# A cosine from one sine with a quarter turn, its rounding on VectorE and its square removed

## The chip, the cores and the metric

One core of one Trainium2 chip runs the whole kernel. The metric is device time in microseconds (us) from one launch; a run's profile gives the span from the first to the last instruction.

## The reference: sliding-window attention feeding g = h cos(h)

Eight batches, 8 heads of 64, 512 local and 32 global tokens. Local queries see the local keys within 32 positions and all global keys; global queries see everything. The result x, 4352 tokens of 512, goes through two products with a cosine between them.

```
s_g = scale * q_g @ [k_g, k_l].T ;  out_g = sm(s_g) @ [v_g, v_l]
s_ll = where(|i - j| <= 32, scale * q_l @ k_l.T, -1e9) ;  s_lg = scale * q_l @ k_g.T
out_l = sm([s_lg, s_ll]) @ [v_g, v_l]
x = concat(out_g, out_l) as (8*544, 512)
h = x @ w_in          # w_in 512 x 2048
g = h * cos(h)
out = g @ w_out       # w_out 2048 x 512
```

## The kernel before

Every fp32 product is formed from fp16 pairs: a value is split into a high half (`xh`, `wi_h`, `gh`, ...) and what is left (`xl`, `wi_l`, `gl`, ...), and three products of halves are summed in PSUM. Powers of two scale each operand, so that the halves fit fp16.

**Attention** is worked for pairs of heads, (batch, pair) from (0,0) to (7,3). PE forms scores `ps` (L573, from batch 3 on L560 with split operands). DVE adds the mask and takes the minimum (L633, tiles `t` and `mn`), ACT takes Exp with sums `sm` (L450), DVE forms reciprocals (L652, L653). ACT writes the high planes (L680) and DVE the low ones (L681), two heads each for four windows. DMA transposes the planes into `pt` (by PE in batch 0). PE sums with the values into `acc` (L733). ACT and DVE evict it as `xh` (L753) and `xl` (L754). Global queries have tiles of their own (`gt`, `planes_g`, `gacc`, `xg`, L796 to L859). Values are split once per batch (`vm` L507, `vl` L538), queries and keys from batch 3 on per pair (`qh` on ACT L614, `qkr` on DVE L617).

**The two products** go by chunks of 256 tokens (16, and one more for the global tokens) and in each by 8 slots of 2x128 hidden columns. A slot has these steps, with the chunk's scales `a`, `m`, `o` in tiny columns (L890 to L894, one set for two chunks):

- `m1_a` (L909): 24 products into the PSUM tile `ph`, three buffers; here h is `ph` times a scale.
- `m1_b`: ACT writes u = ph + m (L931), where m is a large constant that rounds the sum; DVE then forms u = (u - m) - ph (L932), the distance to the nearest period.
- `m1_c`: ACT takes w = Sin(a u) (L937, recorded at L450).
- `m1_d`: GpSimd squares w in four pieces (`pool_tt`, recorded at L238); DVE forms gf = (w - 0.5) ph (L955); ACT casts the high half `gh` (L959); GpSimd forms the low half `gl` in four pieces (L238).
- `m2_a` (L978): 12 products with `w_out` into `po`, which has two buffers, one for each 128 tokens. They come three slots after their `m1_a`, and are called a W_out group below.
- `m2_b`, `m2_c`: after the eighth slot ACT (L989) and DVE (L987) scale `po` into `o`, and a DMA writes it.

So a slot's `ph` is held until gf has read it, and with three `ph` buffers (two slots ahead) the chain u, Sin, square, gf is in the loop that lets PE go on. `w_out` is itself decoded beside the first two chunks: loads into two buffers (`raw_wo`, L427), conversion steps on ACT, DVE and GpSimd (L252, L253, L257, L264, L238) into `wo_hl`.

The order on each engine is set in two steps. The program lists every step under a slot and a phase with `at(...)`, which gives it a priority; a scheduler then simulates the engines with its own costs and fixes one order per engine. A change of one step's engine or length therefore moves steps on all engines. Exp and Sin share ACT, and `table_act` keeps their order, so that function tables are loaded seldom.

```
            nc.scalar.activation(u, ph, AF.Identity, bias=m)                       # L931
            nc.vector.scalar_tensor_tensor(u, u, m, ph, op0=ALU.subtract, ...)     # L932
                pool_tt(w, w, w, ALU.mult, PSQ if c < 2 else PSC)                  # L953
```

Of the kernel before, what the change touches and what calls it, by code (L numbers as in the profile page):

```python
# [145 lines left out]
def body(tc, qf, v, wi, wo, mask, out):  # L146
# [3 lines left out]
    with ExitStack() as ctx:  # L150
# [791 lines left out]
        def m1_d(c, j):  # L942
# [4 lines left out]
            e = SQ[NS * c + j] if c < 2 else "G"  # L947
            if e == "A":
                nc.scalar.activation(w, w, AF.Square)
            elif e == "D":  # L950
                nc.vector.tensor_tensor(w, w, w, op=ALU.mult)
            else:
                pool_tt(w, w, w, ALU.mult, PSQ if c < 2 else PSC)  # L953
# [265 lines left out]
```

## Time and profile before

| | |
|---|---|
| median of 3 runs | 938.96 us (938.77 to 941.5) |
| profiled execution | 938.54 us |
| its span | 936.7 us |
| PE busy | 883.8 us (94%) |
| DVE busy | 648.1 us (69%) |
| ACT busy | 683.0 us (73%) |
| GpSimd busy | 540.6 us (58%) |
| mean granted TensorE clock | 0.966 |

PE is TensorE's products, DVE VectorE, ACT ScalarE, POOL GpSimd. An engine's share is a mean over stages that have different limits, so it is read by stretch: up to about 190 us both weights are decoded and the first two batches' attention runs; then up to about 760 us attention of batches 2 to 7 runs beside the products; after that the products run alone. A line of waits names the engine that stood idle, the tile it was to write, and the instruction that ended last of those it waited for.

### The profile page before, as it was taken

The numbers are of one execution on the slowest core, as the hardware profiler recorded it, in microseconds if no ns is written. First come the engines' busy times: TensorE is split into PE (matmuls) and PEld (weight loads), VectorE is DVE, ScalarE is ACT, GpSimd is POOL, SyncE is SP. The second block draws the span as 40 slices with busy tenths as digits, with TensorE's granted clock in tenths as the row PEclk, the third lists the DMA queues.
The fourth block names the chain that finished last, engine by engine and source line by source line (L and its number), as shares of the span: only waits on it lengthen the run. The fifth ranks groups of instructions, "written<-read, shape, count | busy, mean of one in ns | idle before, by whom it ended". The sixth has DMA issues, their size and how long they took to land.

```text
span 936.7 us, 21428 instructions
## 1 busy us (share of the span) xinstructions
PE 883.8 (94%) x7903; PEld 596.1 (64%) x7903; DVE 648.1 (69%) x1708; ACT 683.0 (73%) x1439; POOL 540.6 (58%) x1228
## 2 busy tenths in 40 slices
PE   6756888999999999999999999999999999999995
PEld 4445554666666666666666666666666666666762
DVE  5999989857576777778877878687776664323231
ACT  6887798876787788877888788788877785434341
POOL 5866968543546555545646364546464556555552
PEclk8568998999999999999999999999999999999998
DMA  9936257555232543545343645362434333000000
GB/s 366 392 140 191 69 145 176 115 116 142 50 104 51 153 85 69 115 125 113 69 112 62 164 61 122 60 175 47 99 67 93 51 69 61 23 1 24 1 23 23
DMA packets 155185, 96.50 MB, mean 103 GB/s; under 512 B 141000, under 2 KB 141128, under 8 KB 153288
## 3 DMA queue, kind: packets, MB, share of 16 engines
q1 hardware_dynamic: 155080, 95.13, 40.4%
q8 instruction: 62, 1.02, 0.4%
q14 instruction: 43, 0.35, 0.1%
HBM read 51.59 MB, written 8.91 MB: 65 GB/s over the span
## 4 chain that ended last, share of the span: by engine, by line
PE 73%; DVE 10%; ACT 6%; DMA 4%; POOL 4%; issue 3%; SPq 0%; ACTq 0%; POOLq 0%
PE ph L909 32%; PE po L978 32%; PE acc L733 3%; PE ps L560 3%; DMA vr<-v 2%; DVE planes L681 2%; ACT t L450 1%; DMA raw_wo<-wo 1%; DVE u L932 1%; PE gacc L838 1%; ACT planes L680 1%; PE gps L783 1%; PE ps L573 1%; DVE gf L955 1%; POOL w L238 1%
## 5 line engine op out<-in xcount | busy, mean ns | idle before, releaser
L238 POOL TENSOR_TENSOR gl<-gf,gh 128x128 f16<-128x128 f32 x544 | 233.2, 463 | 180.6 <-ACT gh L959 180.6
L978 PE MATMUL po<-wo_hl,gh 128*128 128x512 f16 x1088 | 322.3, 381 | 9.6 <-POOL wo_hl L238 9.0
L238 POOL TENSOR_TENSOR w<-w 128x128 f32<-128x128 f32 x544 | 214.4, 426 | 168.6 <-ACT w L450 166.7
L909 PE MATMUL ph<-xh,wi_h 128*128 128x256 f16 x1024 | 280.4, 274 | 3.3 <-DVE gf L955 3.1
L909 PE MATMUL ph<-xl,wi_h 128*128 128x256 f16 x1024 | 279.5, 273 | 0.5 <-DVE xl L754 0.5
L909 PE MATMUL ph<-xh,wi_l 128*128 128x256 f16 x1024 | 279.4, 273 | 0.0
L909 PEld LDWEIGHTS <-wi_h 128*128 128x128 f16 x2176 | 207.3, 98 | 51.6 <-issue 12.7
L978 PE MATMUL po<-wo_hl,gl 128*128 128x512 f16 x544 | 201.5, 381 | 0.0
L978 PEld LDWEIGHTS <-gh 128*128 128x128 f16 x1088 | 106.8, 98 | 103.2 <-issue 2.8
L955 DVE SCALAR_TENSOR_TENSOR gf<-w,ph 128x512 f32<-128x512 f32 x136 | 93.0, 684 | 93.2 <-POOL w L238 92.3
L931 ACT ACTIVATE u<-ph,cm 128x512 f32<-128x512 f32 x136 | 91.7, 678 | 79.0 <-PE ph L909 79.0
L450 ACT ACTIVATE w<-u,ca 128x512 f32<-128x512 f32 x136 | 98.0, 721 | 65.1 <-DVE u L932 57.8
L932 DVE SCALAR_TENSOR_TENSOR u<-u,cm,ph 128x512 f32<-128x512 f32 x136 | 100.7, 740 | 64.6 <-ACT u L931 64.6
L959 ACT CAST gh<-gf 128x512 f16<-128x512 f32 x136 | 83.1, 611 | 55.9 <-DVE gf L955 53.5
L450 ACT ACTIVATE t<-t,mn 128x192 f32<-128x192 f32 (+1 forms) x256 | 116.5, 457 | 6.2 <-DVE mn L633 5.9
L909 PEld LDWEIGHTS <-wi_l 128*128 128x128 f16 x1088 | 106.8, 98 | 13.4 <-issue 0.7
L681 DVE SCALAR_TENSOR_TENSOR planes<-t,sm,planes 128x192 f16<-128x192 f32 (+1 forms) x232 | 95.4, 464 | 6.7 <-ACT planes L680 6.5
L978 PEld LDWEIGHTS <-gl 128*128 128x128 f16 x544 | 53.4, 98 | 73.2 <-issue 11.1
L680 ACT ACTIVATE planes<-t,sm 128x192 f16<-128x192 f32 (+1 forms) x232 | 86.9, 455 | 2.9 <-DVE gsm L810 2.2
L450 ACT ACT_TABLE_LOAD x58 | 74.4, 1283 | 6.7 <-DVE u L932 4.6
L633 DVE CUSTOM_DVE_ANT_0 t<-ps,msk,qs 128x192 f32<-128x192 f32 (+1 forms) x160 | 60.2, 428 | 3.1 <-PE ps L560 3.1
L733 PE MATMUL acc<-pt,vh 128*64 128x128 f16 (+3 forms) x768 | 45.5, 239 | 3.0 <-ACT pt L698 3.0
(173 smaller groups left out, 1116.0 us busy)
## 6 DMA issues: line engine op xcount, KB each, us to landing
qkr<-qf SPq DMA_DIRECT2D x31, 608.0 KB, 5.0
vr<-v SPq DMA_DIRECT2D x8, 1280.0 KB, 6.5
out<-o SPq DMA_DIRECT2D x34, 256.0 KB, 2.0
raw_wi<-wi SPq DMA_DIRECT2D x6, 1024.0 KB, 12.3
wo_hl<-wo SPq DMA_DIRECT2D x8, 512.0 KB, 11.4
raw_wm<-wo SPq DMA_DIRECT2D x8, 512.0 KB, 4.4
raw_wo<-wo SPq DMA_DIRECT2D x8, 512.0 KB, 4.4
raw_wi<-wi SPq DMA_DIRECT2D x4, 512.0 KB, 12.2
```

What stands on the lines that cost most here:

```text
L238: nc.gpsimd.tensor_tensor(o[..., c], a[..., c], b[..., c], op=op)
L450: ins = nc.scalar.activation(*a, **k).ins
L633: nc.vector.tensor_tensor_reduce(t[:, h], pt[h], msk[:, MOFF[i] : MOFF[i] + w], nal, 3.0e38, ALU.add, ALU.min, mn[:, h : h + 1],)
L680: a = nc.scalar.activation(hi, t[:, h], AF.Identity, scale=r)
L681: d = nc.vector.scalar_tensor_tensor(lo, t[:, h], r, hi, op0=ALU.mult, op1=ALU.subtract)
L733: mm = nc.tensor.matmul(acc[64 * h : 64 * h + 64, q_out : q_out + n0 * len(segs)], vt[:, tl, 64 * h : 64 * h + 64], rhs, start=(k == 0 and ...
L909: nc.tensor.matmul(ph[:, a], w[:, kc, f], x[:, kc, q], start=first and ip == 0, stop=last and ip == 2, skip_group_check=True,)
L931: nc.scalar.activation(u, ph, AF.Identity, bias=m)
L932: nc.vector.scalar_tensor_tensor(u, u, m, ph, op0=ALU.subtract, op1=ALU.subtract)
L955: nc.vector.scalar_tensor_tensor(gf, w, 0.5, st.pop(("ph", c, j)).rearrange("p a b -> p (a b)"), op0=ALU.subtract, op1=ALU.mult,)
L959: nc.scalar.copy(gh, gf)
L978: nc.tensor.matmul(po[k], g[:, a * CT + k * P : a * CT + (k + 1) * P], w[:, 2 * j + a], start=(j == 0 and i == 0), stop=(j == NS - 1 and i ...
```

## The change

The cosine is formed by cos(h) = sin(quarter turn - h) in place of 1 - 2 sin(h/2) squared. The rounding goes by whole periods with an offset q of an eighth of m's unit. In order:

- u = (ph + q) + m is one DVE operation that reads PSUM, with two scalar columns; it was an ACT operation. The second pass stays as it was (L933 now).
- Sin has scale -2 pi/period in place of pi/period, and the column `halfpi` as bias. That column is written once at the start; it shares a tile with `pvs`.
- The square is removed, with its constants `PSQ` and `SQ`.
- gf = (-0.5 w) ph in place of (w - 0.5) ph, the same operation with other constants.
- The scales are columns of one tile `cs`, with two more tiny operations per set.

```
--- before.py
+++ after.py
@@ -74,9 +74,7 @@
 LO = "m01v2345"
 J7 = "xl3"
 L7 = -5
-PSQ = 128
 PSG = 128
-SQ = "GGGGGGGGGGGGGGGG"
 GLE = "GGGGGGGGGGGGGGGG"
 WLE = "GGGGGGGGGGGGGGGG"
 WPT = [1, 1, 2, 2, 3, 3, 4, 4, 5, 5, 6, 6, 7, 7, 8, 8]
@@ -183,7 +181,9 @@
         hsc = cp.tile([P, 1], F32, name="hsc")
         osc = cp.tile([P, 1], F32, name="osc")
         xg = cp.tile([P, B, NPAIR, SG], F32, name="xg")
-        pvs = cp.tile([P, B], F32, name="pvs")
+        pvs_hp = cp.tile([P, B + 1], F32, name="pvs_hp")
+        pvs, halfpi = pvs_hp[:, :B], pvs_hp[:, B : B + 1]
+        nc.vector.memset(halfpi, math.pi / 2)
 
         def behind(ins, what, why="scale_first"):
             if st.get(what) is not None:
@@ -884,15 +884,16 @@
                     )
                 st["x", c] = (xh, xl)
 
-            a = ap_.tile([P, 1], F32, tag="ca", name=f"ca_{c}")
-            m = ap_.tile([P, 1], F32, tag="cm", name=f"cm_{c}")
-            o = ap_.tile([P, 1], F32, tag="co", name=f"co_{c}")
+            cs = ap_.tile([P, 4], F32, tag="cs", name=f"cs_{c}")
+            a, m, o, q = (cs[:, i : i + 1] for i in range(4))
             nc.vector.tensor_scalar(a, hsc, pv, None, op0=ALU.mult)
             inv2(m, a)
-            nc.vector.tensor_scalar(m, m, 2.0**90, 0.5 * MAGIC, op0=ALU.min, op1=ALU.mult)
-            nc.vector.tensor_scalar(a, a, math.pi, None, op0=ALU.mult)
+            nc.vector.tensor_scalar(m, m, 2.0**90, None, op0=ALU.min)
+            nc.vector.tensor_scalar(q, m, 0.125, None, op0=ALU.mult)
+            nc.vector.tensor_scalar(m, m, MAGIC / 2, None, op0=ALU.mult)
+            nc.vector.tensor_scalar(a, a, -2.0 * math.pi, None, op0=ALU.mult)
             nc.vector.tensor_scalar(o, osc, pv, None, op0=ALU.mult)
-            st["cs", c] = (a, m, o)
+            st["cs", c] = (a, m, o, q)
 
 
         def m1_a(c, j, part=None):
@@ -928,13 +929,13 @@
                 u = mp.tile([P, n], F32, tag="u", name=f"u_{c}_{j}")
                 w = mp.tile([P, n], F32, tag="w", name=f"w_{c}_{j}")
             m = st["cs", c][1]
-            nc.scalar.activation(u, ph, AF.Identity, bias=m)
+            nc.vector.tensor_scalar(u, ph, st["cs", c][3], m, op0=ALU.add, op1=ALU.add)
             nc.vector.scalar_tensor_tensor(u, u, m, ph, op0=ALU.subtract, op1=ALU.subtract)
             st["u", c, j] = (u, w)
 
         def m1_c(c, j):
             u, w = st["u", c, j]
-            ins = table_act("Sin", w, u, AF.Sin, scale=st["cs", c][0])
+            ins = table_act("Sin", w, u, AF.Sin, scale=st["cs", c][0], bias=halfpi)
             x = st.pop("new_x", None)
             if c and x is not None:
                 tc.add_manual_dep(ins, x.name, order, reason="products_first")
@@ -944,17 +945,10 @@
             n = w.shape[-1]
             gh = mp.tile([P, n], F16, tag="gh", name=f"gh_{c}_{j}", bufs=GB)
             gl = mp.tile([P, n], F16, tag="gl", name=f"gl_{c}_{j}", bufs=GB)
-            e = SQ[NS * c + j] if c < 2 else "G"
-            if e == "A":
-                nc.scalar.activation(w, w, AF.Square)
-            elif e == "D":
-                nc.vector.tensor_tensor(w, w, w, op=ALU.mult)
-            else:
-                pool_tt(w, w, w, ALU.mult, PSQ if c < 2 else PSC)
             gf = gf_tile(c, j, n)
             nc.vector.scalar_tensor_tensor(
-                gf, w, 0.5, st.pop(("ph", c, j)).rearrange("p a b -> p (a b)"),
-                op0=ALU.subtract, op1=ALU.mult,
+                gf, w, -0.5, st.pop(("ph", c, j)).rearrange("p a b -> p (a b)"),
+                op0=ALU.mult, op1=ALU.mult,
             )
             nc.scalar.copy(gh, gf)
             if c < 2 and GLE[NS * c + j] == "D":
```

Three places show what the order does. In names such as `u_1_6_2499` the first numbers are chunk and slot (for `ps`, `t`: batch, pair, window), the last is a count.

On DVE where the products begin, before:

```order
L434 TENSOR_REDUCE wm_o_1010<-wos_108 128x1
L435 TENSOR_SCALAR wm_o_1010<-wm_o_1010 128x1
L932 SCALAR_TENSOR_TENSOR u_0_0_1209<-u_0_0_1209,cm_0_1202,ph_0_0_1038 128x512
L211 TENSOR_SCALAR wm_o_1010<-wm_o_1010 128x1
L932 SCALAR_TENSOR_TENSOR u_0_1_1227<-u_0_1_1227,cm_0_1202,ph_0_1_1045 128x512
```
and with the change:

```order
L932 TENSOR_SCALAR u_0_0_1210<-ph_0_0_1039,cs_0_1202 128x512
L434 TENSOR_REDUCE wm_o_1011<-wos_109 128x1
L932 TENSOR_SCALAR u_0_1_1224<-ph_0_1_1046,cs_0_1202 128x512
L933 SCALAR_TENSOR_TENSOR u_0_0_1210<-u_0_0_1210,cs_0_1202,ph_0_0_1039 128x512
L435 TENSOR_SCALAR wm_o_1011<-wm_o_1011 128x1
L933 SCALAR_TENSOR_TENSOR u_0_1_1224<-u_0_1_1224,cs_0_1202,ph_0_1_1046 128x512
L211 TENSOR_SCALAR wm_o_1011<-wm_o_1011 128x1
```
Each slot has a TENSOR_SCALAR (L932) and a SCALAR_TENSOR_TENSOR (L933) now, and the passes of two slots stand among the scale steps of w_out (`wm_o`).

On DVE at the end of batch 1's attention, where the low planes of pair (1,3) are written, before:

```order
L681 SCALAR_TENSOR_TENSOR planes0_76<-t_1_3_0_2223,sm_1_3_2374,planes0_76 128x192 x2
L681 SCALAR_TENSOR_TENSOR planes1_78<-t_1_3_1_2227,sm_1_3_2374,planes1_78 128x224 x2
L955 SCALAR_TENSOR_TENSOR gf_1_4_2392<-w_1_4_2311,ph_1_4_2285 128x512
L681 SCALAR_TENSOR_TENSOR planes2_80<-t_1_3_2_2237,sm_1_3_2374,planes2_80 128x224 x2
L858 TENSOR_SCALAR xg_97<-gacc_1_0_2331,pvs_98 128x64
L681 SCALAR_TENSOR_TENSOR planes3_82<-t_1_3_3_2241,sm_1_3_2374,planes3_82 128x192 x2
L859 SCALAR_TENSOR_TENSOR xg_97<-gacc_1_0_2331,pvs_98,xg_97 128x64
L816 SCALAR_TENSOR_TENSOR planes_g_84<-gt_1_1_2096,gsm_1_1_2383,planes_g_84 128x544
L538 SCALAR_TENSOR_TENSOR vl_2_1_2685<-vr_2_1620,vs_2_1788,vh_2_1_2684 128x640
L538 SCALAR_TENSOR_TENSOR vl_2_2_3084<-vr_2_1620,vs_2_1788,vh_2_2_3083 128x640
```
and with the change:

```order
L949 SCALAR_TENSOR_TENSOR gf_1_5_2467<-w_1_5_2374,ph_1_5_2348 128x512
L681 SCALAR_TENSOR_TENSOR planes0_76<-t_1_3_0_2180,sm_1_3_2327,planes0_76 128x192 x2
L681 SCALAR_TENSOR_TENSOR planes1_78<-t_1_3_1_2184,sm_1_3_2327,planes1_78 128x224 x2
L681 SCALAR_TENSOR_TENSOR planes2_80<-t_1_3_2_2194,sm_1_3_2327,planes2_80 128x224
L932 TENSOR_SCALAR u_1_7_2570<-ph_1_7_2545,cs_0_1202 128x512
L681 SCALAR_TENSOR_TENSOR planes2_80<-t_1_3_2_2194,sm_1_3_2327,planes2_80 128x224
L681 SCALAR_TENSOR_TENSOR planes3_82<-t_1_3_3_2198,sm_1_3_2327,planes3_82 128x192
L633 ISA t_2_0_2_2528,mn_2_0_2_2529<-ps_2_0_2_0_2515,msk_73 128x224
L633 ISA mn_2_0_2_2529 128x1
L633 ISA t_2_0_2_2528,mn_2_0_3_2532<-ps_2_0_2_0_2515,msk_73 128x192
L633 ISA mn_2_0_3_2532 128x1
L681 SCALAR_TENSOR_TENSOR planes3_82<-t_1_3_3_2198,sm_1_3_2327,planes3_82 128x192
```
The last planes come behind a first pass of slot (1,7) and score passes of batch 2 (`t_2_0`), which came behind two `vl` before; the rows 434 to 442 ahead of the piece shown are four score passes of `t_2_0` and the second pass of slot (1,6).

On PE where the second half of batch 2's first scores (`ps_2_0_2`) stands, before:

```order
L978 LDWEIGHTS gh_1_3_2272
L978 MATMUL po_1_1_2167<-wo_hl_88,gh_1_3_2272 128x512
L573 MATMUL ps_2_0_2_0_2570<-qkr_2_0_1795 128x224
L573 MATMUL ps_2_0_2_1_2571<-qkr_2_0_1795 128x224
L573 MATMUL ps_2_0_2_0_2570<-qkr_2_0_1795 128x192
L573 MATMUL ps_2_0_2_1_2571<-qkr_2_0_1795 128x192
L909 LDWEIGHTS wi_h_86
L909 MATMUL ph_1_7_2604<-xh_0_1026,wi_h_86 128x256
```
and with the change:

```order
L910 LDWEIGHTS wi_l_87
L910 MATMUL ph_1_7_2545<-xh_0_1027,wi_l_87 128x256
L573 MATMUL ps_2_0_2_0_2515<-qkr_2_0_1768 128x224
L573 MATMUL ps_2_0_2_0_2515<-qkr_2_0_1768 128x192
L573 MATMUL ps_2_0_2_1_2516<-qkr_2_0_1768 128x224
L573 MATMUL ps_2_0_2_1_2516<-qkr_2_0_1768 128x192
L972 LDWEIGHTS gh_0_7_1771
L972 MATMUL po_0_0_1344<-wo_hl_88,gh_0_7_1771 128x512
```
Before, W_out products of chunk 1, slot 3 come ahead of these scores (12 groups of 12 products done) and `ph_1_7` behind them. Now `ph_1_7` is ahead of them, and the W_out products that follow are those of chunk 0, slot 7 (7 groups done). So at these scores five W_out groups fewer and one `ph` more are done than before; ahead of the first scores of pair (2,1) both orders have done 15 groups and 18 `ph`.

## Rows read from the trace of the kernel before

**Rows 1.** The page's first two parts: busy time of each engine with its share of the span and its instructions, and PE in 40 slices of 23.4 us in tenths busy.

```profile
PE 883.8 (94%) x7903; PEld 596.1 (64%) x7903; DVE 648.1 (69%) x1708; ACT 683.0 (73%) x1439; POOL 540.6 (58%) x1228
...
PE   6756888999999999999999999999999999999995
```

**Rows 2.** Busy time by stretch. Columns: the stretch and its length in us, then the busy us and number of instructions of PE, PE's weight loads, DVE, ACT and GpSimd, TensorE's granted clock, the DMA share and GB/s.

```profile
86.60:182.00 95.40, 82.05 (x700) 52.69 (x699) 84.19 (x224) 83.79 (x181) 72.14 (x133) 0.95 0.54 141
200.00:926.00 726.00, 725.78 (x6547) 488.04 (x6544) 481.01 (x1241) 516.07 (x1076) 401.52 (x980) 1.00 0.36 79
300.00:700.00 400.00, 399.79 (x3816) 270.43 (x3815) 312.51 (x829) 321.85 (x685) 218.75 (x520) 1.00 0.44 99
```

**Rows 3.** PE's waits from 75 to 200 us: who waited, for what, us in total, times, longest us.

```profile
PE po L978 <- POOL wo_hl L238: 9.0, 5, 3.7
```

**Rows 4.** The chain of waits, in order of time, in the start and at the end. Columns: start us, us, what.

```profile
132.25 5.30 DMA raw_wo<-wo
...
154.66 5.08 DMA raw_wo<-wo
...
184.92 2.73 PE ph L909 x24
187.65 2.59 PE po L978 x12
...
916.01 10.37 PE po L978 x48
```

**Rows 5.** Instructions by line and shape of ACT and then GpSimd, 300 to 700 us, and in the last row GpSimd, 75 to 175 us. Columns: line, engine, operation, out<-in, shapes, count, busy us, mean ns, idle before and what ended it.

```profile
L931 ACT ACTIVATE u<-ph,cm 128x512 f32<-128x512 f32 x64 | 42.8, 675 | 3.8 <-PE ph L909 3.8
...
L238 POOL TENSOR_TENSOR w<-w 128x128 f32<-128x128 f32 x256 | 101.8, 429 | 105.4 <-ACT w L450 105.0
...
L238 POOL TENSOR_TENSOR w<-w 128x128 f32<-128x128 f32 x48 | 20.8, 464 | 7.2 <-ACT w L450 7.2
```

**Rows 6.** DVE's instructions by line and shape, 300 to 700 us, columns as in rows 5.

```profile
L932 DVE SCALAR_TENSOR_TENSOR u<-u,cm,ph 128x512 f32<-128x512 f32 x65 | 48.0, 738 | 21.1 <-ACT u L931 21.1
...
L681 DVE SCALAR_TENSOR_TENSOR planes<-t,sm,planes 128x224 f16<-128x224 f32 x65 | 29.2, 493 | 0.8 <-ACT planes L680 0.8
...
L633 DVE CUSTOM_DVE_ANT_0 t<-ps,msk,qs 128x224 f32<-128x224 f32 x64 | 26.7, 445 | 1.7 <-PE ps L560 1.7
L681 DVE SCALAR_TENSOR_TENSOR planes<-t,sm,planes 128x192 f16<-128x192 f32 x66 | 25.7, 410 | 0.1
...
L538 DVE SCALAR_TENSOR_TENSOR vl<-vr,vs,vh 128x640 f16<-128x640 f32 x16 | 15.4, 980 | 0.0
...
L987 DVE TENSOR_SCALAR o<-po,co 128x512 f32<-128x512 f32 x8 | 6.0, 745 | 2.1 <-PE po L978 2.1
```

**Rows 7.** The same of DVE, 75 to 175 us.

```profile
L955 DVE SCALAR_TENSOR_TENSOR gf<-w,ph 128x512 f32<-128x512 f32 x12 | 8.1, 675 | 0.6 <-POOL w L238 0.6
L681 DVE SCALAR_TENSOR_TENSOR planes<-t,sm,planes 128x224 f16<-128x224 f32 x12 | 7.2, 637 | 0.0
...
L681 DVE SCALAR_TENSOR_TENSOR planes<-t,sm,planes 128x192 f16<-128x192 f32 x12 | 5.7, 509 | 0.6 <-ACT planes L680 0.6
L538 DVE SCALAR_TENSOR_TENSOR vl<-vr,vs,vh 128x640 f16<-128x640 f32 x5 | 5.6, 1172 | 0.0
L633 DVE CUSTOM_DVE_ANT_0 t<-ps,msk 128x224 f32<-128x224 f32 x16 | 5.6, 378 | 0.0
...
L858 DVE TENSOR_SCALAR xg<-gacc,pvs 128x64 f32<-128x64 f32 x2 | 0.5, 272 | 0.0
```

**Rows 8.** The order of time on DVE at both ends of the start and near the end, and in the last row on ACT. Columns: start us, us, engine, line, operation, out<-in, shapes, count, and in brackets the idle time before it and what ended it.

```profile
86.63 0.17 DVE L434 TENSOR_REDUCE wm_o<-wos 128x1 f32<-128x16 f32 x1
86.83 0.15 DVE L435 TENSOR_SCALAR wm_o<-wm_o 128x1 f32<-128x1 f32 x1
...
181.33 0.73 DVE L681 SCALAR_TENSOR_TENSOR planes<-t,sm,planes 128x192 f16<-128x192 f32 x2
...
901.20 0.75 DVE L932 SCALAR_TENSOR_TENSOR u<-u,cm,ph 128x512 f32<-128x512 f32 x1 [0.92 <-ACT u L931]
...
902.04 0.72 ACT L450 ACTIVATE w<-u,ca 128x512 f32<-128x512 f32 x1 [0.37 <-DVE u L932]
```

**Rows 9.** All instructions on the planes tile by DVE, 300 to 700 us: count, shortest, median and longest ns, first and last start.

```profile
L681 DVE SCALAR_TENSOR_TENSOR planes<-t,sm,planes x131: 398/434/678, 303.5 to 699.3; 128x192 f16<-128x192 f32 x66, 128x224 f16<-128x224 f32 x65
```

**Rows 10.** DVE's waits from 300 to 700 us, columns as in rows 3.

```profile
DVE u L932 <- ACT u L931: 21.1, 23, 1.4
DVE gf L955 <- POOL w L238: 17.3, 30, 1.4
DVE sm L652 <- ACT t L450: 17.0, 12, 2.4
DVE qkr L617 <- ACT qh L614: 11.8, 9, 1.3
DVE vm L507 <- DMA vr<-v: 9.4, 4, 2.5
```

**Rows 11.** DVE's waits from 86.6 to 182 us, columns as in rows 3.

```profile
DVE planes L681 <- ACT planes L680: 2.7, 2, 2.0
DVE raw_wo L253 <- DMA raw_wo<-wo: 2.3, 4, 1.0
```

**Rows 12.** All instructions of line L573 (the scores up to batch 2, here those of batch 2) on PE, 185 to 215 us, columns as in rows 9.

```profile
L573 PE MATMUL ps<-qkr x16: 322/349/453, 190.2 to 209.9; 64*128 64x224 f32 x8, 64*128 64x192 f32 x8
```

More of the change, by code (lines that the diff above doesn't have):

```diff
@@ L76 @@
 L7 = -5
-PSQ = 128
 PSG = 128
-SQ = "GGGGGGGGGGGGGGGG"
 GLE = "GGGGGGGGGGGGGGGG"
@@ L185, in body @@
         xg = cp.tile([P, B, NPAIR, SG], F32, name="xg")
-        pvs = cp.tile([P, B], F32, name="pvs")
+        pvs_hp = cp.tile([P, B + 1], F32, name="pvs_hp")
+        pvs, halfpi = pvs_hp[:, :B], pvs_hp[:, B : B + 1]
+        nc.vector.memset(halfpi, math.pi / 2)
         def behind(ins, what, why="scale_first"):
@@ L885, in chunk_scales @@
                 st["x", c] = (xh, xl)
-            a = ap_.tile([P, 1], F32, tag="ca", name=f"ca_{c}")
-            m = ap_.tile([P, 1], F32, tag="cm", name=f"cm_{c}")
-            o = ap_.tile([P, 1], F32, tag="co", name=f"co_{c}")
+            cs = ap_.tile([P, 4], F32, tag="cs", name=f"cs_{c}")
+            a, m, o, q = (cs[:, i : i + 1] for i in range(4))
             nc.vector.tensor_scalar(a, hsc, pv, None, op0=ALU.mult)
             inv2(m, a)
-            nc.vector.tensor_scalar(m, m, 2.0**90, 0.5 * MAGIC, op0=ALU.min, op1=ALU.mult)
-            nc.vector.tensor_scalar(a, a, math.pi, None, op0=ALU.mult)
+            nc.vector.tensor_scalar(m, m, 2.0**90, None, op0=ALU.min)
+            nc.vector.tensor_scalar(q, m, 0.125, None, op0=ALU.mult)
+            nc.vector.tensor_scalar(m, m, MAGIC / 2, None, op0=ALU.mult)
+            nc.vector.tensor_scalar(a, a, -2.0 * math.pi, None, op0=ALU.mult)
             nc.vector.tensor_scalar(o, osc, pv, None, op0=ALU.mult)
-            st["cs", c] = (a, m, o)
+            st["cs", c] = (a, m, o, q)
         def m1_a(c, j, part=None):
@@ L930, in m1_b @@
             m = st["cs", c][1]
-            nc.scalar.activation(u, ph, AF.Identity, bias=m)
+            nc.vector.tensor_scalar(u, ph, st["cs", c][3], m, op0=ALU.add, op1=ALU.add)
             nc.vector.scalar_tensor_tensor(u, u, m, ph, op0=ALU.subtract, op1=ALU.subtract)
@@ L936, in m1_c @@
             u, w = st["u", c, j]
-            ins = table_act("Sin", w, u, AF.Sin, scale=st["cs", c][0])
+            ins = table_act("Sin", w, u, AF.Sin, scale=st["cs", c][0], bias=halfpi)
             x = st.pop("new_x", None)
@@ L946, in m1_d @@
             gl = mp.tile([P, n], F16, tag="gl", name=f"gl_{c}_{j}", bufs=GB)
[L947 to L953, printed above, removed]
             gf = gf_tile(c, j, n)
             nc.vector.scalar_tensor_tensor(
-                gf, w, 0.5, st.pop(("ph", c, j)).rearrange("p a b -> p (a b)"),
-                op0=ALU.subtract, op1=ALU.mult,
+                gf, w, -0.5, st.pop(("ph", c, j)).rearrange("p a b -> p (a b)"),
+                op0=ALU.mult, op1=ALU.mult,
             )
```

## The prediction

> **What bounds the kernel now.** I read the profile in four steps.
>
> First the engine totals and PE's slices [rows 1]. PE is busy 94% of the span. Its slices are 9 tenths from the ninth on (from about 187 us) and lower only in the eight before. So a change that leaves PE's work alone can move two things: how soon PE becomes full, and whether it stays full.
>
> Second, stretches [rows 2]. From 200 to 926 us PE is busy all the time, and in 300 to 700 DVE is busy 312.5 of 400 us, so it has 21.9 us of slack in every 100. In the start, 86.6 to 182 us, it is the other way: DVE works 84.19 of 95.4 us and PE 82.05. There DVE is the fullest engine, with only 11.2 us not busy.
>
> Third, what PE waits for in the start [rows 3]: the low halves of w_out from GpSimd, 9.0 us in five waits. Fourth, the chain of waits [rows 4]: from 187.65 us PE alone carries it, and the end is 48 W_out products in a row, 10.37 us. Before that the chain goes through two loads of w_out, 5.30 and 5.08 us.
>
> The profiled execution took 938.54 us, its span 936.7, so 1.84 us lie around the span. The median is 0.4 above that execution. I sum against 938.54 and add 0.4 at the end.
>
> **What the change does to each engine.** Per slot (512 columns) ACT loses the pass L931, 0.675 us, of which 64 lie in 300 to 700: 10.8 us per 100. GpSimd loses four squares of 0.43 to 0.46 us [rows 5]: 101.8/4 = 25.5 us per 100. DVE gains a first pass from PSUM. Its second pass and gf have the forms they have now. Sin gets a bias pointer; I price that at nothing, because ACT has just been relieved of more than such a pointer could add. If ACT were full, it would cost something in each of 16 slots per 100 us.
>
> **Price of the new DVE pass.** The trace has no TENSOR_SCALAR from PSUM with two scalar pointers. The nearest row has one: o, 128x512 from PSUM, 745 ns [rows 6]; the second pass, SBUF and PSUM in, takes 738. A pointer can add: the score pass takes 445 ns with one and 378 without [rows 6, 7], 67 more, though its elements differ too; so the upper bound is 745 + 55 = 0.80 us. Neighbours overlap: two planes of 0.41 us take 0.73 together [rows 6, 8], 0.09 less than their sum. The lower bound is 0.66. I take **0.70 us**, near the o row less two thirds of that overlap.
>
> The Trainium skill, ScalarE: Activation LUTs, section Rules for kernel authors, says to use VectorE, not ScalarE, for additions, up to about 3 times faster per element in bf16. By it the pass would cost 0.675/3 = 0.23 us (an estimate from that page and a row). The rows speak against it for this operand: 745 ns on DVE, 675 on ACT. The Trainium skill, VectorE: DVE Perf Modes, section Why PSUM operands drop a tier, says fp32 operands in PSUM run at 1x, and the row agrees.
>
> **The full stretch, 200 to 926 us.** DVE: 312.5/4 = 78.1, plus 16.25 x 0.70 = 11.4, less 1.4 for relief from GpSimd, gives 88.1 us per 100. The relief is small, because planes are already near their floor: median 434, shortest 398 ns [rows 9]; 33 planes by some 25 ns, and something from vl. Now the waits [rows 10]. The wait for ACT's u (21.1 us in 400) and for GpSimd's square (17.3) lose their cause. The wait for qh (11.8) should go too, because ACT, which forms qh, loses 10.8 us per 100. What stays per 100: sm 4.25, vm 2.35, and 0.9 for the small ones together. New is gf's wait for Sin: from the end of the second pass to the end of Sin 0.81 us pass [rows 8], and about 0.95 until DVE uses it. The changed order puts other rows between in most slots, as at the second place shown; I keep a quarter of 0.95, 3.7 us per 100. Sum: 88.1 + 4.25 + 2.35 + 0.9 + 3.7 = 99.3. It just fits, so **+0.5 us** for single slips (bounds 0 to +20, rival B).
>
> Two tiny scale operations more per set, 9 sets, at 0.15 us like the tiny row of L435 [rows 8], are 2.7 us over the run, among rows off PE's path. The new constant is written at the start, before DVE has work. The tail gains nothing: of its 48 products [rows 4] only the last groups have late inputs, and PE never waits for them.
>
> **The start.** DVE is the fullest engine, so I follow it from the row L434 at 86.63 us to the last planes of batch 1 at 182 us [rows 8].
> - Its busy time there is now 84.2 us [rows 2].
> - New first passes in this stretch, counted in the order: 15 x 0.70 = +10.5.
> - The order moves work ahead of the last planes: two second passes of u (1.3), a gf (0.6), six score passes (2.2 by the 0.38 row, 1.8 after overlaps), two vl (1.7), an xl (0.66, as the other passes that read PSUM), xg (0.4), less one o (0.67): +5.8 [rows 7].
> - Relief from GpSimd. Planes take 637 and 509 ns here, 493 and 410 later [rows 6, 7], where GpSimd is busy 55% and not 76% [rows 2]. Without the squares it would be (72.1 - 20.8)/95.4 = 54% here. Twelve of each by 144 and 99 ns, and five vl by 192, is 3.9; I take -3, since the low halves stay. Bounds -3.9 to 0.
> - Waits that stay: 11.2 now, of them 2.7 for planes and 2.3 for the load of w_out [rows 11]. I keep 5 (2.3 to 11.2).
>
> The last planes end at 86.6 + 84.2 + 10.5 + 5.8 - 3 + 5 = **189.1 us** (low: 9.9, -3.9 and 2.3 give 184.9; high: 12, 0 and 11.2 give 199.8), against 182 now.
>
> That is not a loss of 7 us, because PE's order changes too, as the third place shows: five W_out groups (2.59 us each [rows 4]) are put behind the scores ps_2_0_2, and one `ph` (24 products, 2.73 us [rows 4]) ahead of them. PE starts these scores at 190.2 us now [rows 12]; the work ahead of them in the new order is due at 190.2 - 12.95 + 2.73 = 180.0. From there PE is full, since the postponed groups have their inputs. It can go on there once DVE has read the four first score tiles of batch 2. DVE's rows from those to the last planes, the second place and one second pass, sum to 6.2 us by [rows 6, 7], and 0.5 pass until PE starts: 189.1 - 5.7 = 183.4. So the start costs 183.4 - 180.0 = **+3.4 us** (-0.8 to +14.1).
>
> **Sum:** 938.54 + 3.4 + 0.5 = 942.4; with 0.4 for the median, **942.8 us**, that is 0.4% slower. A measurement of this kernel tells about 0.3% from no change, so same is 936.1 to 941.8.
>
> **The rivals.**
> - **B, DVE becomes the bound of the full stretch** (951 us). If the qh wait stays (2.95 per 100), DVE needs 99.3 + 2.9 = 102.2 per 100 while attention lasts, 200 to 760 us: 5.6 x 2.2 = 12 us. It decides as soon as the waits that remain exceed 11.9 per 100. For it: DVE gets fullest of all engines beside PE. Against: most waits now are for work that vanishes.
> - **C, faster** (935 us). GpSimd's and ACT's relief is worth more than DVE's load. With the full 3.9 and no waits left, the planes end at 86.6 + 84.2 + 10.5 + 5.8 - 3.9 = 183.2, PE is full at 177.5, 2.5 earlier than due: 938.96 - 2.5 = 936.5, and 1.5 more or so if PE's 9.0 us for low halves [rows 3], which no longer stand behind squares, shrink. If half of them are gone on the path, it is 932. The Trainium skill, SBUF — State Buffer, section Who interferes with whom, says that a DVE instruction with two SBUF inputs contends with a GpSimd instruction that reads SBUF. The planes (637 against 493 ns) agree. Against: DVE, 88% full, gets 12% more work, and only a wait can pay for it.
> - **D, another wait sets the start** (939 us). The loads of w_out, 5.30 and 5.08 us on the chain [rows 4], free buffers and start later work; if they set the pace, DVE's new rows lie in their shadow. For: the chain. Against: DVE waited only 2.3 us for them [rows 11].
> - **E, the first pass is cheap**, 0.23 us, as by the rule on additions: 15 x 0.47 = 7 us less in the start, whose gain ends where GpSimd's and the loads' waits begin, so 935. The o row, 745 ns, speaks against it.
>
> **How the numbers follow.** Forecast 0.43 (936 to 947), B 0.20 (945 to 960), C 0.23 (931 to 936.5), D 0.12, E 0.02. The forecast lies near the edge of what can be told: of its 0.43, 0.24 is slower, 0.18 same, 0.01 faster. Faster: 0.21 of C, 0.02 of E and 0.01 = 0.24. Slower: 0.24, B's 0.20 and 0.01 of D = 0.45. Same: the rest, 0.31. The range of **932 to 952** leaves out B's upper half (0.10) and some 0.08 at both ends of the others.
>
> **What would show it.** Right: the new pass lasts 0.7 to 0.8 us; DVE is over 90% busy from 87 to 185 us; PE becomes full at about 183 us, with W_out groups still owed; in 300 to 700 PE stays at 400 us, DVE rises to about 352, ACT falls by 43 and GpSimd by 102; the end is again 48 products in 10.4 us. Wrong: PE idles in 300 to 700 behind u or gf (B); PE is full by 178 (C); DVE stays below 88% in the start and the loads stay on the chain (D); the new pass takes under 0.5 us (E).

## Result: 0.75% slower, and not for the reason that carried the sum

The changed kernel takes 946.17 us (median of 5, 944.44 to 947.02), before 938.77 us beside it: ratio 1.0075, interval 1.0062 to 1.0089. Its profiled execution took 946.42 us with a span of 944.6. The forecast was 942.8 us, in a range from 932 to 952. Sign and range held, but the two terms of the sum were both wrong and partly made up for each other, so that the total lies in the range is luck.

The page of the changed kernel, its first two parts, beside [rows 1]:

```profile
PE 892.0 (94%) x7903; PEld 601.1 (64%) x7903; DVE 726.9 (77%) x1863; ACT 617.5 (65%) x1303; POOL 338.8 (36%) x684
...
PE   6757999899999999999999999999999999999995
...
DVE  5998989948688888879888888888888876544441
```

Busy time by stretch, columns as in [rows 2]; the first stretch runs from L434 to the last planes of pair (1,3), as the prediction followed it:

```profile
87.33:183.39 96.06, 86.04 (x773) 58.36 (x772) 91.11 (x260) 83.30 (x179) 47.19 (x76) 0.95 0.55 137
200.00:926.00 726.00, 720.67 (x6506) 486.56 (x6504) 558.06 (x1375) 458.48 (x956) 225.16 (x492) 1.00 0.35 79
300.00:700.00 400.00, 394.67 (x3736) 267.21 (x3735) 342.90 (x882) 282.01 (x598) 124.75 (x260) 1.00 0.43 99
```

PE, full in [rows 2], idles 5.3 us in 300 to 700. To see where time is lost, one takes the same PE instruction in both traces. The first product of `acc` for pair (2,0) and for pair (7,0), in the order of time on PE, before and then after (columns as in [rows 8]):

```profile
222.46 0.30 PE L733 MATMUL acc<-pt,vh 128*64 128x128 f16 x4
...
719.41 0.30 PE L733 MATMUL acc<-pt,vh 128*64 128x128 f16 x4
```

```profile
222.14 0.30 PE L733 MATMUL acc<-pt,vh 128*64 128x128 f16 x4
...
727.66 0.30 PE L733 MATMUL acc<-pt,vh 128*64 128x128 f16 x4
```

At (2,0) the changed kernel is 0.32 us ahead: the start costs nothing. At (7,0) it is 8.25 behind. In between the difference moves in steps, one per batch: the first product of pair 1 in batches 2 to 7 comes at -0.32, +0.44, +2.57, +5.74, +8.01 and +8.34 us against before. PE's last product is 8.34 later, and what follows it is 0.45 shorter, which makes the span's 7.9. Below, **start** is the difference to before at (2,0), and **full stretch** what is added from there to PE's last product.

DVE by line and shape, 300 to 700 us (columns as in [rows 6]):

```profile
L932 DVE TENSOR_SCALAR u<-ph,cs 128x512 f32<-128x512 f32 x63 | 50.6, 803 | 0.2
L933 DVE SCALAR_TENSOR_TENSOR u<-u,cs,ph 128x512 f32<-128x512 f32 x63 | 46.8, 743 | 1.0
L949 DVE SCALAR_TENSOR_TENSOR gf<-w,ph 128x512 f32<-128x512 f32 x64 | 43.3, 682 | 22.4 <-ACT w L450 22.2
...
L681 DVE SCALAR_TENSOR_TENSOR planes<-t,sm,planes 128x224 f16<-128x224 f32 x64 | 24.8, 443 | 0.0
```

Sin on ACT in the same stretch:

```profile
L450 ACT ACTIVATE w<-u,pvs_hp,cs 128x512 f32<-128x512 f32 x64 | 51.7, 814 | 38.7 <-DVE u L933 38.1
```

DVE's waits, 300 to 700 us (columns as in [rows 10]), and then PE's from 215 us on:

```profile
DVE gf L949 <- ACT w L450: 22.2, 27, 1.5
DVE sm L652 <- ACT t L450: 17.2, 11, 2.3
DVE vm L507 <- DMA vr<-v: 10.8, 4, 3.7
DVE qkr L617 <- ACT qh L614: 2.4, 3, 0.8
DVE o L981 <- PE po L972: 1.5, 4, 0.8
```

```profile
PE acc L733 <- DVE mn L633: 2.9, 3, 1.5
PE ph L910 <- DVE gf L949: 2.5, 4, 0.8
```

The vm wait existed before (9.4 us). What stands behind it is new. DVE in order of time in the changed kernel, batch 4's scores behind batch 5's values:

```profile
416.53 0.68 DVE L949 SCALAR_TENSOR_TENSOR gf<-w,ph 128x512 f32<-128x512 f32 x1
417.13 0.21 DVE L889 TENSOR_SCALAR cs<-hsc,pvs_hp 128x1 f32<-128x1 f32 x1
417.25 0.20 DVE L895 TENSOR_SCALAR cs<-osc,pvs_hp 128x1 f32<-128x1 f32 x1
420.25 2.82 DVE L507 TENSOR_REDUCE vm<-vr 128x1 f32<-128x2560 f32 x1 [2.79 <-DMA vr<-v]
422.98 0.44 DVE L633 CUSTOM_DVE_ANT_0 t<-ps,msk,qs 128x224 f32<-128x224 f32 x1
```

and before, where the last score pass ends ahead of the same wait:

```profile
416.17 0.44 DVE L633 CUSTOM_DVE_ANT_0 t<-ps,msk,qs 128x224 f32<-128x224 f32 x1
...
417.25 0.41 DVE L633 CUSTOM_DVE_ANT_0 t<-ps,msk,qs 128x192 f32<-128x192 f32 x1
...
420.18 2.82 DVE L507 TENSOR_REDUCE vm<-vr 128x1 f32<-128x2560 f32 x1 [2.44 <-DMA vr<-v]
```

The four score passes begin 6.8 us later, and DVE then works without a pause (of over 0.1 us) until 449 us. Before has such a stretch behind `vm` too, but it ends at 437 us and PE stays full beside it. The stretches in the columns of [rows 2], the changed kernel and then before:

```profile
420.25:449.10 28.85, 27.46 (x237) 17.89 (x237) 28.77 (x78) 18.61 (x41) 8.79 (x17) 1.00 0.45 97
```

```profile
420.18:437.00 16.82, 16.70 (x162) 11.52 (x160) 16.76 (x35) 12.03 (x23) 4.82 (x12) 1.00 0.69 149
```

In every batch from 3 to 6 the order had `vm` behind these passes before and has it ahead of them now.

### The profile page after: what moved, and what is told of

Read it like the earlier page. It is cut to its first block, busy times and chain, and to the rows that moved or that the text cites. A ratio compares the mean times of both kernels' runs of the same rounds, so it can differ in the third digit from the quotient of the medians.

```text
span 944.6 us, 20840 instructions
## 1 busy us (share of the span) xinstructions
PE 892.0 (94%) x7903; PEld 601.1 (64%) x7903; DVE 726.9 (77%) x1863; ACT 617.5 (65%) x1303; POOL 338.8 (36%) x684
## 4 chain that ended last, share of the span: by engine, by line
PE 58%; DVE 13%; ACT 9%; DMA 3%; issue 2%; POOL 0%; ACTq 0%; DVEq 0%
PE po L972 26%; PE ph L910 25%; PE acc L733 3%; ACT planes L680 3%; DMA vr<-v 2%; DVE planes L681 2%; PE ps L560 2%; DVE t L633 2%; ACT L450 2%; ACT w L450 2%; DVE gf L949 2%; DVE u L933 2%; DVE qm L584 1%; DVE u L932 1%; ACT t L450 1%
## 5 line engine op out<-in xcount | busy, mean ns | idle before, releaser
L238 POOL TENSOR_TENSOR gl<-gf,gh 128x128 f16<-128x128 f32 x544 | 242.5, 478 | 532.1 <-ACT gh L953 529.8
L450 ACT ACTIVATE w<-u,pvs_hp,cs 128x512 f32<-128x512 f32 x136 | 109.8, 813 | 124.1 <-DVE u L933 122.7
L932 DVE TENSOR_SCALAR u<-ph,cs 128x512 f32<-128x512 f32 x136 | 109.4, 804 | 46.5 <-PE ph L910 46.3
L933 DVE SCALAR_TENSOR_TENSOR u<-u,cs,ph 128x512 f32<-128x512 f32 x136 | 101.0, 743 | 2.3
L681 DVE SCALAR_TENSOR_TENSOR planes<-t,sm,planes 128x192 f16<-128x192 f32 (+1 forms) x232 | 88.5, 435 | 0.0
L450 ACT ACTIVATION_READ_ACCUMULATOR t<-t,mn 128x1 f32 x256 | 49.0, 191 | 0.0
```

Source lines behind the costliest of these rows:

```text
L238: nc.gpsimd.tensor_tensor(o[..., c], a[..., c], b[..., c], op=op)
L450: ins = nc.scalar.activation(*a, **k).ins
L681: d = nc.vector.scalar_tensor_tensor(lo, t[:, h], r, hi, op0=ALU.mult, op1=ALU.subtract)
L932: nc.vector.tensor_scalar(u, ph, st["cs", c][3], m, op0=ALU.add, op1=ALU.add)
```

## Experiments

All medians stand beside runs of the kernel before on the same chip, where its own median was 938.77 to 939.89 us. DVE is its busy time in 300 to 700 us. Start, full stretch and DVE come from the one profiled execution of each kernel, which took between 1.7 us less (e3) and 3.1 us more (e7) than the median beside it. From 230 to 800 us e2 has the changed kernel's instructions in the changed kernel's order, and its full stretch came out 1.4 us shorter: a difference of that size between two kernels tells nothing.

| kernel | us | ratio to before | start | full stretch | DVE |
|---|---|---|---|---|---|
| before | 938.77 | | 0 | 0 | 312.5 |
| changed | 946.17 | 1.0075 (1.0062 to 1.0089) | -0.3 | +8.7 | 342.9 |
| e1 new in chunks 0, 1 | 938.35 | 0.9996 (0.9987 to 1.0005) | -1.5 | +0.4 | 311.6 |
| e2 new from chunk 2 | 947.77 | 1.0091 (1.0076 to 1.0106) | +2.1 | +7.3 | 343.7 |
| e3 first pass on ACT | 935.38 | 0.9965 (0.9954 to 0.9976) | -3.6 | -0.5 | 306.0 |
| e4 before, first pass on DVE | 950.55 | 1.0121 (1.0106 to 1.0136) | +6.2 | +6.3 | 349.3 |
| e5 vm behind the scores | 941.24 | 1.0021 (1.0010 to 1.0032) | 0.0 | +4.6 | 348.1 |
| e6 both o on ACT | 946.12 | 1.0070 (1.0055 to 1.0085) | -0.9 | +9.0 | 339.0 |
| e7 Sin without bias | 945.67 | 1.0070 (1.0047 to 1.0093) | +3.6 | +7.4 | 344.0 |
| e8 vl on GpSimd | 943.96 | 1.0050 (1.0032 to 1.0067) | +2.1 | +3.5 | 336.0 |
| e9 bound of values on ACT | 943.45 | 1.0055 (1.0038 to 1.0071) | -0.8 | +5.5 | 339.3 |
| e10 e3, batch 1's vl on GpSimd | 943.27 | 1.0047 (1.0028 to 1.0065) | +6.3 | -0.5 | 304.9 |
| e11 e5, qm behind gf | 941.51 | 1.0026 (1.0016 to 1.0035) | -0.6 | +3.5 | 347.3 |
| e12 DVE light | 941.91 | 1.0026 (1.0014 to 1.0037) | +2.4 | +1.8 | 324.6 |

**Where: e1 and e2.** `NEW = 2` chooses by chunk: in e1 chunks below it have the new steps and the rest the old ones, in e2 the reverse.

```
+            if c < NEW:                                    # e2: c >= NEW
                 nc.vector.tensor_scalar(u, ph, st["cs", c][3], m, op0=ALU.add, op1=ALU.add)
+            else:
+                nc.scalar.activation(u, ph, AF.Identity, bias=m)
...
+            if c >= NEW:                                   # e2: c < NEW
+                pool_tt(w, w, w, ALU.mult, PSC)
...                                                       # constants of Sin and gf likewise
```

Expected of e1:

> The new cosine in chunks 0 and 1 alone, the old one (first pass on ACT, square on GpSimd) from chunk 2 on. Theory A (the 7 us are lost in the full stretch from 300 to 700 us, about 2.3 us per batch, and the start costs nothing: in the changed kernel PE stands -0.3 us against before at 222 us): 938.5 us, within 1.5 of the kernel before. Rival S (the start loses and the loss shows late): 944 to 946 us.

Expected of e2:

> The reverse: the old cosine in chunks 0 and 1, the new one from chunk 2 on. Theory A: 945 to 948 us, PE's steps of 2 to 3 us once per batch as in the changed kernel. Rival S: 938 to 940 us.

e1 equals before, and e2 loses what the whole change loses and a little more in its start. The loss lies in the full stretch.

**Which part: e3 and e4.** Each does one of the two parts alone.

```
-            nc.vector.tensor_scalar(u, ph, st["cs", c][3], m, op0=ALU.add, op1=ALU.add)   # e3, from the changed kernel
+            nc.scalar.activation(u, ph, AF.Identity, bias=m)
...
-            nc.scalar.activation(u, ph, AF.Identity, bias=m)                               # e4, from before
+            nc.vector.tensor_scalar(u, ph, m, None, op0=ALU.add)
```

Expected of e3:

> The changed kernel with the first pass of the rounding back on ACT (Identity with the bias m, so the quarter-turn offset of the rounding is left out and the argument of Sin can leave its range); the square stays removed and Sin keeps its bias column. DVE loses 0.8 us per slot, 50.6 us in 300 to 700. Theory D (DVE's own work and its forced waits are the bound of the full stretch): the loss of 8.7 us there is gone, and the start gains, since 15 passes of 0.8 leave it: 930 to 937 us. Rival L (the longer Sin, 814 against 722 ns, lengthens each slot's chain from ph to gf, and PE waits for that): Sin stays, so 943 to 946 us.

Expected of e4:

> The kernel before with one edit: the first pass u = ph + m on DVE. Square on GpSimd and Sin without a bias column stay. Theory D: DVE is as full as in the changed kernel, and gf waits for Sin and the square, so at least as slow: 946 to 960 us. Rival L: Sin is 722 ns again, so the chain is no longer than before: 938 to 942 us.

Both came as theory D had them. The first row is e3 in 300 to 700 us, the second e4:

```profile
300.00:700.00 400.00, 400.00 (x3828) 271.32 (x3826) 305.98 (x837) 329.08 (x687) 123.89 (x268) 1.00 0.44 100
```

```profile
300.00:700.00 400.00, 396.68 (x3779) 269.21 (x3777) 349.31 (x886) 279.88 (x615) 227.49 (x517) 1.00 0.43 98
```

With Sin as long as in the changed kernel (811 ns), e3 keeps PE full for all 400 us, so the loss belongs to the pass on DVE. Removing the square and keeping the pass on ACT beats both kernels: 935.38 us. (e3 leaves out the offset of the rounding, so Sin's argument spans another range.) But e4 has the fuller DVE and loses less in the full stretch than the changed kernel, 6.3 against 8.7: the amount of DVE work alone does not order them. In e4's order `vm` stands behind the scores.

**What behind DVE: e5 to e7.** e5 pins the place of `vm`, e6 takes work off DVE at another place, e7 leaves out the quarter turn.

```
+                if b > 3:                                                            # e5, at vm (L507)
+                    tc.add_manual_dep(r.ins, st["last_t", b - 1, 1].ins.name, order, reason="scores_first")
...
-OV = 2
+OV = 0                                                                               # e6
...
-            ins = table_act("Sin", w, u, AF.Sin, scale=st["cs", c][0], bias=halfpi)
+            ins = table_act("Sin", w, u, AF.Sin, scale=st["cs", c][0])               # e7
```

Expected of e5:

> The changed kernel with one constraint more: from batch 4 on DVE takes the maximum of the next batch's values (vm, which waits 2.8 us for their load) behind the last score passes of pair 1, as the order of before had it, and not ahead of them. DVE has the same instructions. Theory V (a full DVE queue in which the scores stand behind that wait: both are needed): the steps of 2 to 3 us that PE takes once in each of batches 3 to 6 shrink to 1.5 or less, as in the kernel with first pass and square both (1.0 to 1.5 there, vm behind): 939 to 942 us. Theory D (DVE's amount of work and waits alone): the wait is still there, 945 to 947 us. Rival L (the longer Sin): 945 to 947 us.

Expected of e6:

> The changed kernel with both output scalings of a chunk on ACT: DVE loses one operation of 0.75 us per chunk, 1.5 us per batch; vm stays ahead of the scores. Theory D: each us taken from DVE comes back, so 6 us less over four batches: 939 to 941 us. Theory V: the queue behind vm holds nothing of it but the o just ahead, so little: 944 to 947 us. Rival L: 945 to 947 us.

Expected of e7:

> The changed kernel with Sin without its bias column (leaves out the quarter turn, so sine stands for cosine). Sin 722 ns in place of 814. Rival L: the full stretch loses nothing, 938 to 940 us. Theory D: gf's waits for Sin, 22 us in 400, shrink by 27 x 0.09 = 2.4, so at most 0.6 us per batch: 943 to 946 us. Theory V: vm is ahead of the scores, so as D or less: 944 to 946.5 us.

e5 gives back 4.0 of the 8.7 us with the same DVE instructions, as theory V had it. The one constraint moved other steps of DVE's queue as well, second passes and `gf` among them, so the 4.0 us belong to the order that comes with the place of `vm`. e6 takes 4 us of work off DVE in these 400 and gives back nothing, where theory D had 6 us coming back and theory V little. It is not a clean test: with `o` on ACT, DVE's `gf` waits 28.5 us for Sin in place of 22.2, and PE waits 2.2 us for ACT's `o`, a wait that the changed kernel does not have there; DVE's wait at `vm` is 10.0 us, in the changed kernel 10.8. So work taken off DVE need not come back, but what it is worth with ACT left alone e6 does not tell. e7 loses 7.4 us with Sin at 720 ns, so Sin's bias column is a small part at most (rival L falls): the 1.3 us to the changed kernel are within what e2 differs by. Its profiled execution, 948.82 us, was the slowest of its four, 3.1 above their median, so its late start stands for that execution and not for the kernel.

**What is left: e8, e9, e11, e12.** e8 and e9 take work off DVE, e11 moves two more steps behind `gf`, e12 is e8, e9 and e6 together.

```
-VE = [1, 4, 4]
+VE = [1, 4, 1]                                                                       # e8
...
+                    for p in range(4):                                               # e9, b >= 4, in place of L507
+                        junk = mp.tile([P, NT, P], BF16, tag="vj", name=f"vj_{b}_{p}", bufs=1)
+                        nc.scalar.activation(
+                            junk, st["vr", b][:, p], AF.Abs, accum_out=m4[:, p : p + 1]
+                        )
+                    nc.vector.tensor_reduce(m, m4, axis=AX.X, op=ALU.max)
...
+            n = b + 1 if p == 3 else b                                               # e11, at qm (L584), on top of e5
+            if p in (3, 0) and 4 <= n < 8:
+                tc.add_manual_dep(r.ins, st["gf", 2 * n - 4, 3].ins.name, order, reason="gf_first")
```

Expected of e8:

> The changed kernel with the low halves of the values formed on GpSimd from batch 2 on (ACT scales the values in place and copies the high half): DVE loses four operations of 1.0 us per batch, and in the order that results vm stands behind the scores. Theories D and V both: the loss of the full stretch is gone, 936 to 940 us. Rival L: 944 to 947 us.

Expected of e9:

> The changed kernel with the batch's bound on its values taken by ACT from batch 4 on (sums of magnitudes of four pieces in place of DVE's maximum of 2.82 us; DVE keeps one tiny maximum of the four sums, which stands behind the scores). With vm only moved behind the scores the full stretch still lost 4.6 of 8.7 us, and DVE worked without a pause for some 20 us behind the load. Theory V2 (the backlog that the 2.8 us of waiting and the 2.8 us of vm leave on a DVE with no slack, whatever stands directly behind it): both are gone from DVE, so the full stretch loses under 1.5 us: 937 to 939.5 us. Theory V (only the scores behind vm): as with vm moved, 941 us. Rival P (each slot's first pass has to queue on DVE, at any place of the batch): 941 to 944 us.

e8 missed all expectations: +2.1 us in the start, which is another order, and 3.5 us of the loss left. e9 missed V2's and came as rival P had it (943.45 us, 941 to 944 expected): without `vm` on DVE no more is won than with `vm` moved. But V2's condition was met in part only, since DVE's small maximum now waits 4.7 us for ACT, and `sm` waits 24.2 us for ACT in place of 17.2. e9's rows show the next thing that is late. DVE in order of time (the column of the idle time is empty: no pause), and PE behind it:

```profile
530.55 1.41 DVE L593 TENSOR_REDUCE qm<-qkr 128x1 bf16<-128x1216 f32 x1
531.88 0.41 DVE L690 SCALAR_TENSOR_TENSOR planes<-t,sm,planes 128x192 f16<-128x192 f32 x1
532.21 0.74 DVE L942 SCALAR_TENSOR_TENSOR u<-u,cs,ph 128x512 f32<-128x512 f32 x1
532.87 1.48 DVE L626 SCALAR_TENSOR_TENSOR qkr<-qkr,qs,qh 128x1216 f16<-128x1216 f32 x1
534.26 1.41 DVE L593 TENSOR_REDUCE qm<-qkr 128x1 bf16<-128x1216 f32 x1
535.59 0.14 DVE L819 TENSOR_SCALAR gsm<-gsm 128x1 f32<-128x1 f32 x1
535.65 1.27 DVE L958 SCALAR_TENSOR_TENSOR gf<-w,ph 128x512 f32<-128x512 f32 x2
```

```profile
536.38 0.27 PE L919 MATMUL ph<-xh,wi_h 128*128 128x256 f16 x1 [0.93 <-DVE gf L958]
```

Two `gf` go at once, so the first was overdue; its `ph` buffer is what PE waits for.

Expected of e11:

> The kernel with vm behind the scores, and two more steps put in another place of DVE's queue in batches 3 to 6: the two maxima of queries and keys (qm, 1.41 us each) behind gf of the batch's fourth slot and behind the split qkr. Where vm was moved or taken off DVE, gf of that slot stood behind low planes, both qm and qkr, some 9 us without a pause, though its sine was long ready, and PE waited 0.9 us for it and up to 1.3 us more in the scores ahead. DVE's amount of work stays. Theory Q (the order of the queue in that stretch, not the amount): the full stretch loses 2 us or less, against 4.6 with vm moved alone: 937.5 to 940 us. Rival P (each first pass has to queue, anywhere): as with vm moved, 941 to 942 us.

Theory Q missed: the full stretch lost 3.5 us and not 2 or less, and the total came as rival P had it (941 to 942 us). The step between the first products of pair 0 and pair 1, +2.1 us in batch 5 with e5, became -0.3. But 0.8 to 1.9 us per batch were now lost between pairs 2 and 3 in batches 4 to 6, and the median is that of e5 (941.51 and 941.24 us). The wait moved within the batch.

Expected of e12:

> The changed kernel with everything moved off DVE that the single moves took: from batch 4 on the bound of the values on ACT, from batch 2 on the low halves of the values on GpSimd, and both output scalings on ACT. Each slot's first pass stays on DVE. DVE's busy time in 300 to 700 should fall from 343 to some 318 us, near the 312 of the kernel before; ACT rises to some 310. Theory D, as a threshold (what is left of the loss comes from DVE having too little slack, wherever the steps stand): the full stretch loses under 1.5 us. Rival P (a first pass that has to queue on DVE costs at any load): it still loses 3.5 us or more. The start may move by some us either way with the order, so the two are told apart by PE's accumulations from 222 us on, not by the total (935 to 944 us).

```profile
300.00:700.00 400.00, 400.00 (x3834) 271.98 (x3829) 324.63 (x874) 313.21 (x674) 138.27 (x312) 1.00 0.43 99
```

With every first pass still on DVE and 325 us of work, PE is full, so rival P falls; theory D missed its bound of 1.5 us by a little. The 1.8 us that remain lie in the score products, with no wait of PE: 400 of them in 300 to 700 us take 26.1 us here and 24.3 before. Half of them stand in groups of 7 and 18 here (0.68 and 1.19 us on the mean) and of 10 and 15 before (0.68 and 0.97); why the same products take longer so was not tested. So 305 to 325 us of DVE work in 400 let PE stay full, 336 to 349 do not, and in between nothing was run.

Among the fuller ones the busy time does not order the losses, but DVE's longest stretch without a pause of over 0.1 us (300 to 740 us) nearly does. It is 15.6 to 17.0 us in before, e1, e3, e10 and e12 (full stretch -0.5 to +1.8), 18.2 to 21.9 in e5, e8, e9 and e11 (+3.5 to +5.5), 24.0 in e4 (+6.3) and 28.9 to 29.2 in the changed kernel, e2, e6 and e7 (+7.3 to +9.0). This order was found in the traces afterwards; no run set that length alone, and e9, with 18.2 us and +5.5, stands out of line.

**The start: e10.** One constant on top of e3: `VE = [1, 1, 4]`. For batch 1 ACT then scales the values and copies their high halves, and GpSimd forms the low ones.

Expected of e10:

> The kernel with the first pass on ACT and the square removed (935.4 us), and batch 1's low halves of the values on GpSimd, which has lost its squares: DVE loses four operations of some 1.0 us in the start, where it is the fullest engine. If DVE bounds the start, 2 to 4 us less: 932 to 934 us. If its order or ACT bounds it, 934.5 to 938 us.

Both expectations missed. Four DVE operations less made the start 9.9 us later than e3's, and the median 7.9 us. PE waited 9.0 us for low halves of w_out there (4.5 in e3) and 4.2 for `gf` (0.9). The trace also shows that the moved step frees the buffer of the values later: the load of batch 2's values is issued at 117.89 us, in e3 at 107.94, and `vm` of batch 2 begins at 124.86 us, in e3 at 114.59. Whether PE's delay comes from that, no run tests.

Over all these kernels the start lies between -3.6 and +6.3 us. The order differs from kernel to kernel, but so do the executions: those of one kernel lie up to 4.7 us apart (e7, 944.16 to 948.82). The granted TensorE clock of 75 to 200 us differs too: 0.91, 0.94 and 0.94 in e4, e10 and e2, which start 6.2, 6.3 and 2.1 us late, 0.97 and 0.99 in e3 and e1, which are 3.6 and 1.5 ahead, and 0.98 in e8, which does not fit (2.1 late); in 300 to 700 us it is 1.00 in all. What part of a kernel's start is its DVE work, its order, or the clock, these runs do not tell.

## Why the prediction was right in sign and wrong in its terms

- **The price of the pass** held. Its row says 803 ns, just above the bound of 0.80, but that is from start to end, and the next step begins before the end. Where DVE has no pause, `gf` follows a first pass 0.73 us after its start, against the 0.70 that was taken net of such overlap:

```profile
437.25 0.80 DVE L932 TENSOR_SCALAR u<-ph,cs 128x512 f32<-128x512 f32 x1
437.98 0.67 DVE L949 SCALAR_TENSOR_TENSOR gf<-w,ph 128x512 f32<-128x512 f32 x1
```

  e4 prices the second column: the same operation with one column takes 738 ns there, so 65 more, as the 67 of the score passes suggested. Rival E had 0.23 us; it falls.
- **Sin's bias column was priced at nothing**, and takes 92 ns (722 to 814, and 720 again in e7). The Trainium skill, ScalarE: Activation LUTs, section What ACT_TABLE_LOAD costs, states about 93 ns for each such operand; the trace agrees. The step named ACT's slack as its cover, but the cost falls on the chain: DVE's `gf` waits for Sin, 5.6 us per 100 where 3.7 were kept (a quarter of 0.95 in 16.25 slots is 3.9). In time it is worth little: e7, without the column, loses 7.4 us in the full stretch, the changed kernel 8.7.
- **The start, +3.4 forecast, -0.3 measured.** The last planes ended at 183.4 us, not 189.1. The waits left were right (96.06 - 91.11 = 4.95, 5 kept). The busy time was not: 91.1 against 84.2 + 10.5 + 5.8 - 3 = 97.5. The relief was the term mis-sized. In 75 to 175 us, changed kernel:

```profile
L538 DVE SCALAR_TENSOR_TENSOR vl<-vr,vs,vh 128x640 f16<-128x640 f32 x7 | 6.4, 933 | 0.0
L681 DVE SCALAR_TENSOR_TENSOR planes<-t,sm,planes 128x192 f16<-128x192 f32 x12 | 5.9, 523 | 0.0
...
L681 DVE SCALAR_TENSOR_TENSOR planes<-t,sm,planes 128x224 f16<-128x224 f32 x12 | 5.0, 454 | 0.0
```

  The wider planes fell by 183 ns and vl by 239 against [rows 7], the narrow planes not at all. Taken apart by what each step adds behind the step before it, from L434 to the last planes: the first passes add 10.9 us (10.5 taken) and the moved steps some 6.1 (5.8). Planes and vl take 4.6 less, the steps that decode w_out 3.8 less (L253 on raw_wo falls from 594 to 420 ns, L257 with wo_hl from 815 to 721), and small steps 1.7 less. So the relief was some 10 us where 3 were taken, and the decode steps were not in the sum at all; whether GpSimd's squares cause all of it, no run isolates. The planes ended at 183.4 us, as rival C had it (183.2), with more relief than C's 3.9 and with the waits kept. PE began ps_2_0_2 at 178.47 us where 180.0 was due, and had lost 1.2 of that gain by 222; its waits between sum to 0.3 us, so most of the 1.2 may lie in the estimate of what was due.
- **The full stretch, +0.5 forecast, +8.7 measured.** This is the step that failed: "It just fits". The waits were foreseen well but for `gf`: u and square gone, sm 4.3 per 100 (4.25), vm 2.7 (2.35), qkr down to 0.6, `gf` 5.6 (3.7), DVE busy 85.7 (88.1). But a mean of 99.3 in 100 says nothing of the stretch in which the work comes. In each batch DVE stood 1.5 to 3.7 us at `vm` and then had 28.9 us without a pause (16.5 to 16.8 before), and what PE needed was in that queue. The prediction kept the vm wait as a wait that "stays" and did not ask who stands behind it, though the order of the changed kernel shows the score passes there.
- **Rival B** named the right place and side, and 12 us of loss, with the wrong cause: the qh wait went, from 11.8 us to 2.4. It had 0.20, and 946.17 us lies in its range (945 to 960) as well as in the forecast's (936 to 947).
- **Luck.** The start came 3.7 us under its term and the full stretch 8.2 over; only the sum of the two lies near the forecast.
- One reading was a slice off: the eighth of PE's slices in [rows 1] is a 9 too, so they are 9 from about 164 us. No term rests on it.

Shown by runs: the loss is that of the first pass on DVE in chunks from 2 on (e1 to e3), an order with `vm` behind the scores takes back 4.0 of the 8.7 us (e5), and with 325 us of DVE work PE has no wait left in 300 to 700 us (e12), though 1.8 us remain. Argued from rows, not shown: that it is the length of the stretch without a pause that counts. Open: whether another order could hold PE full with 340, and what moves the start.

## What to carry to other kernels

A busy share near what fits is no forecast for an engine whose order is fixed: take the longest stretch without a pause and compare it with that of the kernel before, and ask at each wait that stays which instructions stand behind it in the new order. Price every per-partition column on the chain of a loop, even on an engine with slack. And where a scheduler re-plans, compare kernels at the same instruction on the full engine, stretch by stretch, since one stretch's order can hide another's gain.

## What the runs showed of the hardware

- A [128,1] operand costs Sin of 512 elements 92 ns on ACT (722 to 814) and TENSOR_SCALAR of 512 elements from PSUM 65 ns on DVE (738 to 803).
- The low planes read two SBUF tiles on DVE. In 300 to 700 us their mean over both widths is 451 to 458 ns in the three kernels that keep GpSimd's squares there (before, e1, e4) and 425 to 430 in the eleven without. In before the wide ones pay (493 ns against 443 in the changed kernel), in e4 the narrow ones as well (449 against 410). The Trainium skill, SBUF — State Buffer, section Who interferes with whom, states that a DVE instruction with two SBUF inputs contends with a GpSimd instruction that reads SBUF. The traces agree in that stretch; in 75 to 175 us the wide planes fall from 637 to 454 ns and the narrow ones do not (509 and 523).
